# Top-k attention feeding a squared-ReLU feed-forward: half-batch order, 256-row chunks and a contiguous score layout

## The chip, the cores and the metric

The kernel runs on 1 core of one Trainium2 chip. The metric is the device time of one execution in microseconds, as the median of the runs; lower is better.

## The reference

There are 8 batches, 8 heads, 576 positions and a head dimension of 64. Scores are `q k^T / 8`. In each row of 576 scores only those at or above the 32nd largest stay, a softmax runs over them, and the result multiplies `v`. The heads are put side by side into rows of 512 (4608 rows in all), which go through `relu(x @ w_in)^2 @ w_out`, with 2048 hidden columns.

```python
scores = scale * np.matmul(q, k.transpose(0, 1, 3, 2))
kth = np.partition(scores, -top_k, axis=-1)[..., -top_k:-top_k + 1]
scores = np.where(scores >= kth, scores, -1e9)
attn = softmax(scores)
x = (attn @ v).transpose(0, 2, 1, 3).reshape(B * S, H * D)
r = np.maximum(x @ w_in, 0.0)
out = (r * r) @ w_out
```

## The kernel before

**Groups.** Two heads make a pair (four pairs `hp` in a batch). A group is 128 query rows of both heads of one pair, `g` = 0 to 3, or, as group `Z`, the last 64 query rows of two pairs. A batch has 18 groups, the run has 144.

**One group** (`top_k`, L495, then `attend`, L640). PE makes the scores (`scores`, L503, or `scores_z`, L516) into the three PSUM banks of the pool `ps_s`, of which there is one. ACT copies them to SBUF, tile `s`, in two copies (L533 and L535): in PSUM the last 64 keys of both heads lie in the third bank, in SBUF between the two heads. DVE takes the maximum `m` of the two halves of a row (L589: one operand from PSUM, one from SBUF) and the maximum of the halves of `m` (L594, called `big`). POOL makes the matching minima with four integer adds and subtracts (`whole`, L585, shown at L586): `t1`, `t2`, `mid` and `low`. DVE then takes three rounds of 8 maxima and a replacement of them, over 104, 124 and 272 columns (L609, L613), and a last MAX8 over all 576 columns (L616), which gives the 32nd largest, `kth`. ACT makes `w` from `s` and `kth` (L624); PE transposes `s` and adds `w` times a steep constant in two steps (`flip`, L644), so that what is below `kth` goes far negative; ACT takes the exponential of all 1152 columns (L657).

**Groups into rows** (`collect`, L661). PE multiplies by `v`, ACT copies, DVE takes reciprocals (L685), POOL scales (L687), PE transposes, ACT copies into a tile `xt` (or `xz`) of the feed-forward's input (L711). `stages` says which groups of a pair are collected together.

**Feed-forward** (`feed`, L717). A chunk is a list of row ranges in `CHUNKS` (L413 to L419). It starts when the last of its rows has been collected. For a chunk of `nt` rows, `kf = 512 // nt` hidden blocks share one PSUM bank; PE multiplies with `win` (`fh`), ACT takes ReLU (L737), and the square is taken on DVE in the last chunk (L745), on POOL in the chunks that L747 names (L748), on ACT elsewhere (L751). Then PE multiplies 128 rows at a time with `wo` (`fo`), ACT copies (L768), SP stores (L776). Chunks of before: two of 256 rows in batch 0; 512 rows each in batches 1 to 5; 384 rows of all `Z` groups of batches 0 to 5; 512 rows of batch 6; 384 rows of batch 6's `Z`, rows 256 to 511 and the `Z` of batch 7; then 128 and 128 rows of batch 7.

**Order** (`batch_order`, L396). In batch 0 the groups 0 and 1 of all pairs come first, then 2 and 3. In batches 1 to 6 a pair's four groups come together, with a `Z` after every second pair's. In batch 7 `Z` comes first, then groups 2, 3, 0 and 1.

**Planner.** Every instruction group is an `Op` with an engine, an assumed duration and a priority. `schedule` (L120) is a list scheduler: at each moment each engine takes, of what is ready and has its buffers, the smallest priority; `nbf` is an earliest time. Each engine then runs its list in order, with semaphore waits. Priorities come from `tg = T0 + PER * n` for group `n`: scores at `tg - LEAD`, `m` at `tg - ME`, `big` at `tg - MQ`, POOL's `t2` and `mid` at `tg - MP`, the feed-forward at its chunk's time plus `LAG` (`LAGL` in the last batch), in steps of `STEP`. Buffers: 6 of `s`, 3 of `m`, 4 of `f`, 5 of `qk` (the transposed q and k of a pair), 5 of `vb`, and 2 PSUM banks (`psum`) for everything that is neither scores nor transposed scores.

Of the kernel before, what the change touches and what calls it, by code (L numbers as in the profile page):

```python
# [12 lines left out]
P = 128  # L13
# [278 lines left out]
def bass_top_k_attn__then__act_relu_squared_kernel(  # L292
# [20 lines left out]
    def sb(name, shape, dt=FP32, n=None):  # L313
# [13 lines left out]
    LAGL = 10  # L327
    WARM = 0

    ident32 = sb("ident32", [P, P])  # L330
# [24 lines left out]
        "av": ([P, 4, D + 1], FP32, 3), "x": ([P, 4, D], BF16, 2), "xt": ([P, NCT, 512], BF16, 3),  # L355
        "xz": ([P, NCT, 64 * (NB - 2)], BF16, 1), "o": ([P, DM], FP32, 2),
# [9 lines left out]
    ps32 = nc.alloc_psum_tensor("ps", [P, 8, 512], FP32)  # L366
    ps16 = ps32[:, :, :].bitcast(BF16)

    ps_s, ps_e, psum = Pool("ps_s", 1), Pool("ps_e", 1), Pool("psum", 2)
    BASE = {"ps_s": 0, "ps_e": 3, "psum": 6}  # L370

    def tile(nm):
        return Tile(pools[nm])

    def at(t):
        return mem[t.pool.name][t.slot]
# [17 lines left out]
    Z = 4  # L394

    def batch_order(b):  # L396
        if b == 0:
            seq = []
            for gs in ((0, 1), (2, 3)):
                seq += [(hp, g) for hp in range(NHP) for g in gs]  # L400
            return seq + [(0, Z), (2, Z)], [[0, 1], [2, 3]]
        if b < NB - 1:
            seq = []
# [9 lines left out]
    CHUNKS = [[(0, 0, 256)], [(0, 256, 256)]]  # L413
    for b in range(1, NB - 2):
        CHUNKS.append([(b, 0, 512)])
    CHUNKS.append([(b, 512, 64) for b in range(NB - 2)])
    CHUNKS.append([(NB - 2, 0, 512)])
    CHUNKS.append([(NB - 2, 512, 64), (NB - 1, 256, 256), (NB - 1, 512, 64)])
    CHUNKS += [[(NB - 1, 0, 128)], [(NB - 1, 128, 128)]]  # L419
# [7 lines left out]
    def mm(o, l, r, start, stop=True):  # L427
        return pe.matmul(o, l, r, start=start, stop=stop, skip_group_check=True)  # L428
# [4 lines left out]
    def build(full, weights, pl):  # L433
# [7 lines left out]
        def load_pair(b, hp, base):  # L441
# [11 lines left out]

            def loadv():
                r = at(rv)
                res = [nc.sync.dma_start(r[:, 4 * h:4 * h + 4, :], v[b, 2 * hp + h, 0:512, :].rearrange(
                    "(tb p) d -> p tb d", p=P)) for h in range(2)]

                for h, low, e in ((0, 0, 8), (1, 64, 9), (1, 0, 10) if hp % 2 == 0 else (0, 64, 11)):
                    res.append(nc.sync.dma_start(r[low:low + 64, e, :], v[b, 2 * hp + h, 512:576, :]))  # L460
# [34 lines left out]
        def top_k(gi, qks, tg):  # L495

            n = state["n"]
            state["n"] += 1
            ss, st = Tile(ps_s), tile("s")

            def scores():  # L503
                o = wide(ss)
                for h, to, c0, n_ in ((0, 1024, 512, 64), (0, 0, 0, 512), (1, 512, 0, 512), (1, 1088, 512, 64)):
                    x = at(qks[h])
                    if to == 1088:
                        pe.wait_ge(fence, fences[0])
                    ins = mm(o[:, to:to + n_], x[64 * h:64 * h + 64, 0, 128 * gi:128 * gi + 128],
                             x[64 * h:64 * h + 64, 1, c0:c0 + n_], to != 1088)  # L510
                    if to == 1024:
                        fences[0] += 1
                        ins.then_inc(fence, 1)
                return ins

            def scores_z():  # L516
                o = wide(ss)
                for i in range(2):
                    x = at(qks[i])
                    for to, c0, n_, first in ((1024 + 64 * i, 512, 64, i == 0), (512 * i, 0, 512, True)):  # L520
                        for h in range(2):
                            ins = mm(o[64 * h:64 * h + 64, to:to + n_], x[64 * h:64 * h + 64, 0, 512:576],
                                     x[64 * h:64 * h + 64, 1, c0:c0 + n_], first)
                return ins

            qu = sorted(set(qks), key=lambda t: t.num)
            pl.op("pe", 1.25 if gi != Z else 1.4, tg - LEAD, scores if gi != Z else scores_z, r=qu, w=[ss], take=[ss, st])


            def flat():  # L530
                return at(st)[:, :, :].rearrange("p i c -> p (i c)")

            cp = [pl.op("act", 1.1, tg - LEAD + 1, lambda: act.copy(  # L533
                two(flat(), 640, 512), two(wide(ss), 512, 512)), r=[ss], w=[st]),
                pl.op("act", .35, tg - LEAD + 1, lambda: act.copy(  # L535
                    flat()[:, 512:640], wide(ss)[:, 1024:1152]), r=[ss], w=[st])]

            dk = [0]

            def dve(dur, fn, dp=0, **kw):  # L540
                dk[0] += 1
                return pl.op("dve", dur, tg + .33 * dk[0] + dp, fn, **kw)
# [38 lines left out]
            else:  # L581
# [135 lines left out]
        def feed(chunk, xt, tm, step):  # L717
# [74 lines left out]
        for b in range(NB):  # L792
# [3 lines left out]
            for hp, gi in seq:  # L796
# [179 lines left out]
```

## Time and profile before

| what | us |
|---|---|
| median of 3 runs (lowest to highest) | 933.46 (932.37 to 939.02) |
| the profiled execution's own time | 930.32 |
| its span, first to last instruction | 928.2 |

The profiled execution lies 2.1 us above its span and 3.1 us under the median. Times below are microseconds from the start of the span. Busy is the union of an engine's instructions; the mean of a group is the length of one instruction, and neighbours overlap a little, so that sums of means are more than busy time. PEclk is the share of full TensorE clock that was granted.

### The profile page before, as it was taken

How to read it: one execution, taken by the hardware profiler on the slowest of the kernel's cores; microseconds unless marked ns; L12 is line 12 of the kernel's file. 1: busy time of each engine (PE TensorE's matmuls, PEld its weight loads, DVE VectorE, ACT ScalarE, POOL GpSimd, SP SyncE). 2: the span in 40 equal slices, each digit the busy share in tenths (PEclk: the TensorE clock that was granted, in tenths of full speed). 3: DMA queues.
4: the chain of work that ended last, by engine and by line, in shares of the span. 5: the costliest groups of instructions: out<-in, count | busy, mean ns of one | idle time of the engine just before them, and what ended most of it. 6: DMA issues, size and time to landing. Idle time of an engine off the chain costs nothing.

```text
span 928.2 us, 20946 instructions
## 1 busy us (share of the span) xinstructions
PE 810.1 (87%) x7253; PEld 565.7 (61%) x7330; DVE 864.2 (93%) x3269; ACT 742.8 (80%) x1277; POOL 750.3 (81%) x794
## 2 busy tenths in 40 slices
PE   5766889997689999888888898888998999999996
PEld 4555567766465666656566666656666655665664
DVE  3999999999999999999999999999999999998931
ACT  3665898987699878997799977998779789787762
POOL 6998988878777888777877887877899986899961
PEclk9898999999899999999999999999999999999999
DMA  6742521034101222111210131111211010000101
GB/s 138 190 129 91 141 54 53 14 88 91 39 6 37 53 51 63 27 29 49 58 45 16 40 89 37 41 39 39 52 38 26 13 37 13 24 13 1 43 27 38
DMA packets 126978, 48.11 MB, mean 52 GB/s; under 512 B 119184, under 2 KB 119184, under 8 KB 126864
## 3 DMA queue, kind: packets, MB, share of 16 engines
q1 hardware_dynamic: 125664, 46.39, 19.8%
q8 instruction: 59, 0.97, 0.4%
q14 instruction: 55, 0.45, 0.2%
q10 hardware_dynamic: 1200, 0.30, 0.2%
HBM read 37.22 MB, written 9.44 MB: 50 GB/s over the span
## 4 chain that ended last, share of the span: by engine, by line
DVE 45%; PE 35%; ACT 14%; issue 3%; DMA 1%; POOL 1%; SPq 0%; DVEq 0%
PE ps L428 27%; DVE f L613 13%; DVE kth L616 10%; DVE c L609 10%; PE ps L431 9%; DVE m L589 6%; DVE f L594 5%; ACT p L657 5%; ACT w L624 3%; ACT s L533 2%; ACT g L737 1%; ACT g L751 1%; DMA rq<-in_q_dram 1%; ACT xt L711 0%; ACT qk L488 0%
## 5 line engine op out<-in xcount | busy, mean ns | idle before, releaser
L613 DVE MATCH_REPLACE8 f<-c,f 128x104 f32<-128x104 f32 (+2 forms) x864 | 267.2, 317 | 0.4 <-issue 0.3
L609 DVE MAX8 c<-f 128x8 f32<-128x104 f32 (+2 forms) x864 | 243.7, 321 | 0.1
L428 PE MATMUL ps<-qk 64*128 64x64 f32 (+3 forms) x1280 | 213.9, 454 | 32.8 <-DVE m L589 31.6
L624 ACT ACTIVATE w<-s,kth 128x576 bf16<-128x576 f32 x288 | 222.3, 782 | 6.2 <-DVE kth L616 6.1
L586 POOL TENSOR_TENSOR t<-s 128x576 int32<-128x576 int32 x144 | 203.1, 1413 | 17.7 <-ACT s L535 17.6
L431 PE MATMUL ps<-ident,s 128*128 128x128 f32 x1296 | 200.2, 283 | 16.0 <-ACT w L624 15.4
L533 ACT COPY s<-ps 128x1024 f32<-128x1024 f32 x144 | 146.5, 1017 | 84.2 <-PE ps L428 83.8
L616 DVE MAX8 kth<-f 128x8 f32<-128x576 f32 x288 | 203.4, 748 | 1.6 <-POOL f L586 1.6
L586 POOL TENSOR_TENSOR f<-t,f 128x288 int32<-128x288 int32 x144 | 114.4, 795 | 110.8 <-DVE f L594 94.7
L586 POOL TENSOR_TENSOR f<-t,m 128x576 int32<-128x576 int32 x144 | 202.7, 1408 | 0.0
L428 PEld LDWEIGHTS ps<-qk 64*128 64x128 f32 (+1 forms) x1280 | 129.2, 180 | 110.2 <-DVE m L589 48.1
L657 ACT ACTIVATE p<-ps 128x1152 bf16<-128x1152 f32 x144 | 162.9, 1131 | 33.5 <-PE ps L428 32.6
L431 PEld LDWEIGHTS ps<-ident,s 128*128 128x128 f32 x1296 | 147.0, 143 | 50.1 <-ACT w L624 21.1
L428 PE MATMUL ps<-xt,win 128*128 128x512 bf16 (+3 forms) x674 | 126.8, 324 | 13.7 <-ACT g L737 7.4
L428 PE MATMUL ps<-wo,g 128*128 128x512 bf16 x529 | 134.2, 379 | 4.5 <-ACT xt L711 1.2
L589 DVE TENSOR_TENSOR m<-ps,s 128x576 f32<-128x576 f32 x144 | 107.5, 747 | 19.3 <-ACT s L535 16.9
L428 PE MATMUL ps<-steep_bf,w 128*128 128x128 bf16 x1296 | 121.4, 221 | 0.0
L586 POOL TENSOR_TENSOR t<-m 128x288 int32<-128x288 int32 x144 | 115.1, 799 | 0.0
L594 DVE TENSOR_REDUCE f<-m 128x288 f32<-128x576 f32 x144 | 106.7, 747 | 0.1
L737 ACT ACTIVATE g<-ps 128x512 bf16<-128x512 f32 (+1 forms) x152 | 87.2, 581 | 20.2 <-PE ps L428 19.7
L428 PEld LDWEIGHTS ps<-steep_bf,w 128*128 128x128 bf16 x1296 | 98.4, 99 | 3.6
L428 PEld LDWEIGHTS ps<-xt,win 128*128 128x128 bf16 x704 | 57.7, 98 | 51.8 <-ACT g L737 11.8
(57 smaller groups left out, 774.6 us busy)
## 6 DMA issues: line engine op xcount, KB each, us to landing
rq<-in_q_dram SPq DMA_DIRECT2D x64, 128.0 KB, 2.5
rv<-in_v_dram SPq DMA_DIRECT2D x64, 128.0 KB, 2.4
rk<-in_k_dram SPq DMA_DIRECT2D x62, 128.0 KB, 2.6
out_dram<-o SPq DMA_DIRECT2D x31, 256.0 KB, 2.1
g<-in_moe_w_in_dram SPq DMA_DIRECT2D x8, 512.0 KB, 4.7
g<-in_moe_w_out_dram SPq DMA_DIRECT2D x8, 512.0 KB, 3.9
rv<-in_v_dram SPq DMA_DIRECT2D x96, 16.0 KB, 2.2
out_dram<-o SPq DMA_DIRECT2D x10, 128.0 KB, 2.4
```

The lines of the kernel that those rows point to most:

```text
L428: return pe.matmul(o, l, r, start=start, stop=stop, skip_group_check=True)
L431: return pe.matmul(o, i, ident, is_transpose=True, skip_group_check=True, **kw)
L533: cp = [pl.op("act", 1.1, tg - LEAD + 1, lambda: act.copy(two(flat(), 640, 512), two(wide(ss), 512, 512)), r=[ss], w=[st]), pl.op("act", . ...
L586: return pl.op("gp", dur, prio, lambda: gp.tensor_tensor(o().bitcast(I32), x().bitcast(I32), y().bitcast(I32), op), **kw)
L589: dve(.67, lambda: vec.tensor_tensor(at(m)[:, :, :], two(wide(ss), 736, HALF), two(flat()[:, HALF:], HALF, HALF), ALU.max), dp=-ME, r=[ss] ...
L594: big = dve(.67, lambda: vec.tensor_reduce(at(f)[:, :, 0:QUART], at(m)[:, :, :].rearrange("p i (a c) -> p i c a", a=2), AX.X, ALU.max), dp ...
L609: lambda i=i, t=t, c0=c0, c1=c1: vec.max(eighth(t, i), at(f)[:, i, c0:c1]),
L613: lambda i=i, t=t, c0=c0, c1=c1: vec.match_replace(at(f)[:, i, c0:c1], eighth(t, i), at(f)[:, i, c0:c1], NEG), hold=[f])]
L616: ks.append(chain(kth, i, prev[i] + [low], .665, lambda i=i: vec.max(eighth(kth, i), at(f)[:, i, :]), hold=[f]))
L624: pl.op("act", .77, tw + .8 * i, lambda i=i: act.activation(at(wt)[:, i, :], at(st)[:, i, :], ACTF.Relu, bias=kth[:, i, n:n + 1], scale=-1.0),
L657: pl.op("act", 1.15, tt + 1, lambda: act.activation(at(pt)[:, :, :].rearrange("p k q -> p (k q)"), wide(e), ACTF.Exp, scale=0.125), r=[e], ...
L737: return act.activation(at(g)[:, 0:kf * nt], bank(hh)[:, 0:kf * nt], ACTF.Relu)
```

## The change

The order of batches 0 to 6 becomes groups 0 and 1 of all pairs, then 2 and 3 with a `Z` behind every second pair. Chunks become 256 rows (half a batch over all heads), the `Z` rows of four batches make a chunk of 256, and batch 7's groups 2 and 3 are collected together. The scores of a pair stand in PSUM as in SBUF, 1152 columns in a row: head 0 in columns 0 to 575, head 1 in 576 to 1151. So one ACT copy takes the place of two, and the block of 64 and 64 keys that the heads share is now head 0's last and head 1's first keys (loads of `v` follow). The four products are issued alternately for head 0 and head 1: 64 and 128 columns, then 512 and 448, the last behind the fence. `M1` is 0, so the branch under it makes no instructions. The squares go to POOL in batch 7 and for 2 of the 8 tiles of other chunks, to ACT for the rest. The planner's numbers are others.

```diff
-    PER = 6.0
-    LEAD = 20
-    ME = 10
-    MQ = 0
-    MP = 3
-    LAG = 20
-    STEP = 3.2
-    LATE = 1.5
-    LAGL = 10
+    PER = 5.54
+    LEAD = 8.16
+    ME = 11.99
+    MQ = 9.97
+    MP = 1.61
+    SQ = 1.19
+    M1 = 0
+    LAG = 26.67
+    STEP = 3.08
+    LATE = .69
+    LAGL = 17.1
...
-"xt": ([P, NCT, 512], BF16, 3), "xz": ([P, NCT, 64 * (NB - 2)], BF16, 1)
+"xt": ([P, NCT, 256], BF16, 4), "xz": ([P, NCT, 256], BF16, 2)
...
         if b < NB - 1:
-            seq = []
+            seq = [(hp, g) for hp in range(NHP) for g in (0, 1)]
             for hp in range(NHP):
-                seq += [(hp, g) for g in range(4)]
-                if hp % 2 == 0:
-                    seq.append((hp, Z))
+                seq += [(hp, 2), (hp, 3)] + ([(hp - 1, Z)] if hp % 2 else [])
             return seq, [[0, 1], [2, 3]]
-        seq = [(0, Z), (2, Z)] + [(hp, g) for g in (2, 3) for hp in range(NHP)]
-        return seq + [(hp, g) for g in (0, 1) for hp in range(NHP)], [[0], [1], [2], [3]]
+        seq = [(0, Z), (2, Z)] + [(hp, g) for hp in range(NHP) for g in (2, 3)]
+        return seq + [(hp, g) for g in (0, 1) for hp in range(NHP)], [[0], [1], [2, 3]]
...
+    CHUNKS = []
+    for b in range(NB):
+        if b < NB - 1:
+            CHUNKS += [[(b, 0, 256)], [(b, 256, 256)]]
+        if b % 4 == 3:
+            CHUNKS.append([(b - 3 + i, 512, 64) for i in range(4)])
+    CHUNKS += [[(NB - 1, 256, 256)], [(NB - 1, 0, 128)], [(NB - 1, 128, 128)]]
...
-                for h, to, c0, n_ in ((0, 1024, 512, 64), (0, 0, 0, 512), (1, 512, 0, 512), (1, 1088, 512, 64)):
+                for h, to, c0, n_ in ((0, 512, 512, 64), (1, 1024, 448, 128), (0, 0, 0, 512), (1, 576, 0, 448)):
...
-            cp = [pl.op("act", 1.1, tg - LEAD + 1, lambda: act.copy(
-                two(flat(), 640, 512), two(wide(ss), 512, 512)), r=[ss], w=[st]),
-                pl.op("act", .35, tg - LEAD + 1, lambda: act.copy(
-                    flat()[:, 512:640], wide(ss)[:, 1024:1152]), r=[ss], w=[st])]
+            cp = [pl.op("act", 1.2, tg - LEAD + 1, lambda: act.copy(
+                at(st)[:, :, :].rearrange("p i c -> p (i c)"), wide(ss)), r=[ss], w=[st])]
...
-                elif b >= NB - 2 or (b == NB - 3 and len(chunk) > 1):
+                elif last or i * SQ % 8 < SQ:
                     pl.op("gp", ...
```

## Rows read from the trace of the kernel before

**Rows 1.** The page, part 1: engine, busy us, share of the span, instructions.
```profile
PE 810.1 (87%) x7253; PEld 565.7 (61%) x7330; DVE 864.2 (93%) x3269; ACT 742.8 (80%) x1277; POOL 750.3 (81%) x794
```

**Rows 2.** By stretch: length, busy PE, PEld, DVE, ACT, POOL, PEclk, DMA, GB/s.
```profile
400.00:500.00 100.00, 88.91 (x804) 61.66 (x813) 100.00 (x377) 85.68 (x146) 80.12 (x81) 1.00 0.17 42
...
800.00:850.00 50.00, 48.34 (x428) 33.15 (x433) 45.70 (x178) 41.62 (x76) 45.77 (x51) 1.00 0.03 12
850.00:900.00 50.00, 48.21 (x385) 30.62 (x390) 36.88 (x145) 34.28 (x66) 45.81 (x53) 1.00 0.06 22
```

**Rows 3.** DVE's waits from 800 to 900: us in total, times, longest.
```profile
DVE rzall L685 <- ACT av L683: 9.1, 3, 4.2
DVE f L613 <- POOL f L586: 4.1, 5, 1.9
DVE m L589 <- POOL f L586: 2.0, 2, 1.7
DVE kth L616 <- POOL f L586: 1.6, 1, 1.6
```

**Rows 4.** POOL's instructions by line and shape: count, busy us, mean ns.
```profile
L586 POOL TENSOR_TENSOR t<-s 128x576 int32<-128x576 int32 x144 | 203.1, 1413 | 17.7 <-ACT s L535 17.6
L586 POOL TENSOR_TENSOR f<-t,m 128x576 int32<-128x576 int32 x144 | 202.7, 1408 | 0.0
...
L586 POOL TENSOR_TENSOR t<-m 128x288 int32<-128x288 int32 x144 | 115.1, 799 | 0.0
L586 POOL TENSOR_TENSOR f<-t,f 128x288 int32<-128x288 int32 x144 | 114.4, 795 | 110.8 <-DVE f L594 94.7 <-DVE rzall L685 15.7
...
L748 POOL TENSOR_TENSOR g<-g 128x384 bf16<-128x384 bf16 x32 | 26.3, 832 | 3.6 <-ACT g L737 3.6
...
L748 POOL TENSOR_TENSOR g<-g 128x512 bf16<-128x512 bf16 x20 | 20.7, 1039 | 10.6 <-ACT g L737 10.5
```

**Rows 5.** POOL from 887 to 898, in order of time: start, us, and idle before.
```profile
887.07 3.19 POOL L748 TENSOR_TENSOR g<-g 128x384 bf16<-128x384 bf16 x4
...
896.34 1.40 POOL L586 TENSOR_TENSOR f<-t,m 128x576 int32<-128x576 int32 x1
```

**Rows 6.** ACT by line and shape: the two copies of scores, and the exponential.
```profile
L657 ACT ACTIVATE p<-ps 128x1152 bf16<-128x1152 f32 x144 | 162.9, 1131 | 33.5 <-PE ps L428 32.6
...
L533 ACT COPY s<-ps 128x1024 f32<-128x1024 f32 x144 | 146.5, 1017 | 84.2 <-PE ps L428 83.8
...
L535 ACT COPY s<-ps 128x128 f32<-128x128 f32 x144 | 40.7, 282 | 0.0
```

**Rows 7.** PE in order of time: 256-column products, 512-column products, one group's scores.
```profile
132.84 1.92 PE L428 MATMUL ps<-xt,win 128*128 128x256 bf16 x16 [0.79 <-ACT g L737]
...
401.58 1.89 PE L428 MATMUL ps<-xt,win 128*128 128x512 bf16 x8
...
410.10 1.35 PE L428 MATMUL ps<-qk 64*128 64x64 f32 x8 [0.23 <-DVE m L589]
```

**Rows 8.** PE from 800 to 900 by line and shape: the feed-forward's products.
```profile
L428 PE MATMUL ps<-wo,g 128*128 128x512 bf16 x104 | 25.8, 379 | 1.0 <-ACT s L535 0.6
...
L428 PE MATMUL ps<-xt,win 128*128 128x512 bf16 x59 | 15.2, 379 | 0.7 <-ACT av L683 0.4
...
L428 PE MATMUL ps<-xt,win 128*128 128x384 bf16 x64 | 12.4, 327 | 0.6 <-ACT g L737 0.6
```

**Rows 9.** The end, in order of time: the last kth, last product with v, last chunk.
```profile
897.77 1.42 DVE L616 MAX8 kth<-f 128x8 f32<-128x576 f32 x2 [1.59 <-POOL f L586]
...
903.41 1.13 ACT L657 ACTIVATE p<-ps 128x1152 bf16<-128x1152 f32 x1 [0.24 <-PE ps L428]
...
910.24 0.48 PE L428 MATMUL ps<-vb,p 128*128 128x65 bf16 x10
...
914.19 3.75 PE L428 MATMUL ps<-xt,win 128*128 128x128 bf16 x64
...
921.43 0.58 ACT L768 COPY o<-ps 128x512 f32<-128x512 f32 x1 [2.86 <-PE ps L428]
```

More of the change, by code (lines that the diff above doesn't have):

```diff
@@ L303, in bass_top_k_attn__then__act_relu_squared_kernel @@
     HALF, QUART = S // 2, S // 4
+    REST = (512, 0)
     NHP = 4
@@ L316, in sb @@
         return [nc.alloc_sbuf_tensor(f"{name}{i}", shape, dt) for i in range(n)]
-    PER = 6.0
+    PER = 5.54
     T0 = 12.0
-    LEAD = 20
-    ME = 10
-    MQ = 0
-    MP = 3
-    LAG = 20
-    STEP = 3.2
-    LATE = 1.5
-    LAGL = 10
+    LEAD = 8.16
+    ME = 11.99
+    MQ = 9.97
+    MP = 1.61
+    MA = 12
+    SQ = 1.19
[4 more added lines that the diff above has]
+    LAGL = 17.1
     WARM = 0
@@ L354, in bass_top_k_attn__then__act_relu_squared_kernel @@
         "sh": ([P, 2], FP32, 2), "w": ([P, 2, S], BF16, 4), "p": ([P, 9, 128], BF16, 4),
-        "av": ([P, 4, D + 1], FP32, 3), "x": ([P, 4, D], BF16, 2), "xt": ([P, NCT, 512], BF16, 3),
-        "xz": ([P, NCT, 64 * (NB - 2)], BF16, 1), "o": ([P, DM], FP32, 2),
+        "av": ([P, 4, D + 1], FP32, 3), "x": ([P, 4, D], BF16, 2), "xt": ([P, NCT, 256], BF16, 4),
+        "xz": ([P, NCT, 256], BF16, 2), "o": ([P, DM], FP32, 2),
     }
@@ L367, in bass_top_k_attn__then__act_relu_squared_kernel @@
     ps16 = ps32[:, :, :].bitcast(BF16)
-    ps_s, ps_e, psum = Pool("ps_s", 1), Pool("ps_e", 1), Pool("psum", 2)
-    BASE = {"ps_s": 0, "ps_e": 3, "psum": 6}
+    ps_s, ps_q, ps_e, psum = Pool("ps_s", 1), Pool("ps_q", 1), Pool("ps_e", 1), Pool("psum", 2)
+    BASE = {"ps_s": 0, "ps_q": 2, "ps_e": 3, "psum": 6}
     def tile(nm):
@@ L396, in batch_order @@
     def batch_order(b):
-        if b == 0:
-            seq = []
-            for gs in ((0, 1), (2, 3)):
-                seq += [(hp, g) for hp in range(NHP) for g in gs]
-            return seq + [(0, Z), (2, Z)], [[0, 1], [2, 3]]
         if b < NB - 1:
-            seq = []
+            seq = [(hp, g) for hp in range(NHP) for g in (0, 1)]
             for hp in range(NHP):
-                seq += [(hp, g) for g in range(4)]
-                if hp % 2 == 0:
-                    seq.append((hp, Z))
+                seq += [(hp, 2), (hp, 3)] + ([(hp - 1, Z)] if hp % 2 else [])
             return seq, [[0, 1], [2, 3]]
-        seq = [(0, Z), (2, Z)] + [(hp, g) for g in (2, 3) for hp in range(NHP)]
-        return seq + [(hp, g) for g in (0, 1) for hp in range(NHP)], [[0], [1], [2], [3]]
[L413 to L419, printed above, removed]
+        seq = [(0, Z), (2, Z)] + [(hp, g) for hp in range(NHP) for g in (2, 3)]
[7 more added lines that the diff above has]
+    CHUNKS += [[(NB - 1, 256, 256)], [(NB - 1, 0, 128)], [(NB - 1, 128, 128)]]
     def two(ap, step, n_):
@@ L455, in loadv @@
                 r = at(rv)
-                res = [nc.sync.dma_start(r[:, 4 * h:4 * h + 4, :], v[b, 2 * hp + h, 0:512, :].rearrange(
+                res = [nc.sync.dma_start(r[:, 4 * h:4 * h + 4, :], v[b, 2 * hp + h, 64 * h:64 * h + 512, :].rearrange(
                     "(tb p) d -> p tb d", p=P)) for h in range(2)]
                 for h, low, e in ((0, 0, 8), (1, 64, 9), (1, 0, 10) if hp % 2 == 0 else (0, 64, 11)):
-                    res.append(nc.sync.dma_start(r[low:low + 64, e, :], v[b, 2 * hp + h, 512:576, :]))
+                    res.append(nc.sync.dma_start(r[low:low + 64, e, :], v[b, 2 * hp + h, REST[h]:REST[h] + 64, :]))
                 return res
@@ L498, in top_k @@
             state["n"] += 1
-            ss, st = Tile(ps_s), tile("s")
+            ss, st, sq = Tile(ps_s), tile("s"), Tile(ps_q)
             def scores():
                 o = wide(ss)
-                for h, to, c0, n_ in ((0, 1024, 512, 64), (0, 0, 0, 512), (1, 512, 0, 512), (1, 1088, 512, 64)):
+                for h, to, c0, n_ in ((0, 512, 512, 64), (1, 1024, 448, 128), (0, 0, 0, 512), (1, 576, 0, 448)):
                     x = at(qks[h])
-                    if to == 1088:
+                    if to == 576:
                         pe.wait_ge(fence, fences[0])
                     ins = mm(o[:, to:to + n_], x[64 * h:64 * h + 64, 0, 128 * gi:128 * gi + 128],
-                             x[64 * h:64 * h + 64, 1, c0:c0 + n_], to != 1088)
-                    if to == 1024:
+                             x[64 * h:64 * h + 64, 1, c0:c0 + n_], to != 576)
+                    if to == 512:
                         fences[0] += 1
@@ L517, in scores_z @@
                 o = wide(ss)
-                for i in range(2):
+                for i, runs in ((0, [((512, 512, 64), (0, 0, 512)), ((512, 0, 64), (0, 64, 512))]),
+                                (1, [((1024, 384, 128), (576, 512, 64), (640, 0, 384)),
+                                     ((1024, 448, 128), (576, 0, 448))])):
                     x = at(qks[i])
-                    for to, c0, n_, first in ((1024 + 64 * i, 512, 64, i == 0), (512 * i, 0, 512, True)):
+                    for k_ in range(3):
                         for h in range(2):
-                            ins = mm(o[64 * h:64 * h + 64, to:to + n_], x[64 * h:64 * h + 64, 0, 512:576],
-                                     x[64 * h:64 * h + 64, 1, c0:c0 + n_], first)
+                            if k_ < len(runs[h]):
+                                to, c0, n_ = runs[h][k_]
+                                ins = mm(o[64 * h:64 * h + 64, to:to + n_], x[64 * h:64 * h + 64, 0, 512:576],
+                                         x[64 * h:64 * h + 64, 1, c0:c0 + n_], not 576 <= to < 1024)
                 return ins
             qu = sorted(set(qks), key=lambda t: t.num)
-            pl.op("pe", 1.25 if gi != Z else 1.4, tg - LEAD, scores if gi != Z else scores_z, r=qu, w=[ss], take=[ss, st])
-            def flat():
-                return at(st)[:, :, :].rearrange("p i c -> p (i c)")
-            cp = [pl.op("act", 1.1, tg - LEAD + 1, lambda: act.copy(
-                two(flat(), 640, 512), two(wide(ss), 512, 512)), r=[ss], w=[st]),
-                pl.op("act", .35, tg - LEAD + 1, lambda: act.copy(
-                    flat()[:, 512:640], wide(ss)[:, 1024:1152]), r=[ss], w=[st])]
+            pl.op("pe", 1.25 if gi != Z else 1.4, tg - LEAD, scores if gi != Z else scores_z, r=qu,
+                  w=[ss] + ([sq] if M1 else []), take=[ss, st] + ([sq] if M1 else []))
+            cp = [pl.op("act", 1.2, tg - LEAD + 1, lambda: act.copy(
+                at(st)[:, :, :].rearrange("p i c -> p (i c)"), wide(ss)), r=[ss], w=[st])]
             dk = [0]
@@ L587, in whole, with parts, quarter @@
                         o().bitcast(I32), x().bitcast(I32), y().bitcast(I32), op), **kw)
-                dve(.67, lambda: vec.tensor_tensor(
-                    at(m)[:, :, :], two(wide(ss), 736, HALF), two(flat()[:, HALF:], HALF, HALF), ALU.max),
-                    dp=-ME, r=[ss], hold=[st], after=cp, w=[m], take=[m])
+                def parts(a, n_):
+                    return two(wide(ss)[:, a:], S, n_), at(st)[:, :, HALF + a:HALF + a + n_]
+                def quarter():
+                    return two(ps32[:, 2, 128:416], QUART, QUART)
+                if M1:
+                    m1 = dve(.36, lambda: vec.tensor_tensor(quarter(), *parts(QUART, QUART), ALU.max), dp=-ME,
+                             r=[ss], hold=[st, sq], after=cp)
+                    m0 = dve(.36, lambda: vec.tensor_tensor(at(m)[:, :, 0:QUART], *parts(0, QUART), ALU.max), dp=-ME,
+                             r=[ss], hold=[st], after=cp, w=[m], take=[m])
+                    mc = pl.op("act", .45, tg - MA, lambda: act.copy(at(m)[:, :, QUART:HALF], quarter()), hold=[sq],
+                               w=[m], after=[m1, m0])
+                    big = dve(.36, lambda: vec.tensor_tensor(
+                        at(f)[:, :, 0:QUART], at(m)[:, :, 0:QUART], quarter(), ALU.max), dp=-MQ,
+                        hold=[m, sq], after=[m0, mc], w=[f], take=[f])
+                else:
+                    dve(.67, lambda: vec.tensor_tensor(at(m)[:, :, :], *parts(0, HALF), ALU.max), dp=-ME,
+                        r=[ss], hold=[st], after=cp, w=[m], take=[m])
+                    big = dve(.67, lambda: vec.tensor_reduce(
+                        at(f)[:, :, 0:QUART], at(m)[:, :, :].rearrange("p i (a c) -> p i c a", a=2), AX.X, ALU.max),
+                        dp=-MQ, r=[m], w=[f], take=[f])
                 whole(1.38, tg, ALU.add, lambda: at(t1)[:, :, :], lambda: at(st)[:, :, 0:HALF],
                       lambda: at(st)[:, :, HALF:S], r=[st], w=[t1], take=[t1])
-                big = dve(.67, lambda: vec.tensor_reduce(
-                    at(f)[:, :, 0:QUART], at(m)[:, :, :].rearrange("p i (a c) -> p i c a", a=2), AX.X, ALU.max),
-                    dp=-MQ, r=[m], w=[f], take=[f])
                 whole(.77, tg - MP, ALU.add, lambda: at(t2)[:, :, :], lambda: at(m)[:, :, 0:QUART],
@@ L812, in build @@
                 if first:
-                    xts[i] = tile("xz" if len(CHUNKS[i]) > 4 else "xt")
+                    xts[i] = tile("xz" if len(CHUNKS[i]) > 1 else "xt")
                 collect(gi, held[hp, js[0]], (xts[i], col, first), hp, tt)
```

## The prediction

> **What bounds the kernel now.** I read the page's busy shares first, then busy time by stretch, then DVE's waits in the stretches where it is not full, then the other engines there. The reader is to see three things.
>
> First, DVE is the fullest engine, 864.2 us of 928.2 [rows 1], and from 400 to 500 it is busy for the whole 100.00 us [rows 2]; PE, ACT and POOL have 11, 14 and 20 us free there. So in the middle the time is the number of DVE instructions, and what the other engines do is hidden. 864.2 over 144 groups is 6.0 us for a group.
>
> Second, the last batch is otherwise. DVE is busy for 45.70 us from 800 to 850 and 36.88 from 850 to 900 [rows 2], so 17.4 us are idle. Its waits there [rows 3] are 4.1 + 2.0 + 1.6 = 7.7 us for POOL by name, and 9.1 us at reciprocals. These last are POOL's too: the reciprocals stand in DVE's queue ahead of the last MAX8, and that MAX8 still waits 1.59 us afterwards [rows 9] for POOL's subtraction at 896.34, which ran behind a block of four squares at 887.07 and others like it [rows 5]. POOL is busy for 45.77 and 45.81 of 50 us there and PE for 48.34 and 48.21 [rows 2].
>
> Third, the end. The last MAX8 ends at 899.19; the last exponential ends at 904.54, but its product with `v` starts only at 910.24, since PE is working through feed-forward products; the last chunk starts at 914.19 and its copy ends at 922.01 [rows 9]. From the last MAX8 to the end of the span are 29.0 us.
>
> **The change part by part.**
>
> *DVE.* No instruction is added or taken away, as `M1` is 0. `m` still reads two runs of 288 columns from the first two banks. I cost it at 0. `big` gets priority 9.97 us earlier, behind `m`. POOL's `mid` waits for `big`: 94.7 us of POOL's idle time stand there [rows 4]. That idle goes, but in the middle it costs DVE little.
>
> *Score copy.* Two copies of 1017 and 282 ns become one of 1152 columns; the nearest row is the exponential, 1131 ns over the same three banks [rows 6]. ACT gains between 0 (if the two overlap fully at their ends) and 0.168 us for a group, 24 us in all, and I take 0 on the path, since DVE hides it. At the very start the first group gains 0.1 us. If the cover were gone, it could only help.
>
> *Scores interleaved.* One group now takes 1.35 us on PE [rows 7]: a 64-column product, two of 512 on different rows of the array, a 64-column product. Now 64 stands beside 128 and 512 beside 448. Between a gain of 0.25 us (one small product wholly hidden) and a loss of 0.25 us (the fence now stands ahead of a long product, with the transposes of the group before queued behind it) I take a gain of 0.1, 2 us for the last batch's 18 groups. In the middle it hides behind DVE: PE waits for DVE's `m` before scores anyway, 0.23 us in that row.
>
> *256-row chunks.* The first product runs 16 x 256 columns in 1.92 us where before it ran 8 x 512 in 1.89 [rows 7]: nothing lost. `wo`'s products, copies and stores keep their number. The order by half batches holds a pair's `qk` for 13 to 18 groups rather than 5. With five buffers, the fifth holds the next batch's first pair, two come free after group 13 of 18 and two at the batch's end, and the next batch needs them from its 3rd and 7th group; the number of loads on SP's queue is the same. I cost that at 0, with up to 1 us at each of 7 batch ends as the other end.
>
> The Trainium skill, "TensorE: Matmul & The Clock Gate", section "The mechanism", says that a weight load overlaps with running products only where the row group differs; these all use all rows. By that, twice the loads of 98 ns would be exposed, 32 more in a chunk of 256, 3.1 us a chunk and some 10 us in the last batch, and the sum would end near 926. The rows speak against it: 120 ns for a product of 256 columns leaves no room for a load beside it.
>
> *Squares.* Before, POOL squares all tiles of the chunks fed in batch 7, 30.6 us between 800 and 900 (14.5 + 13.0 + 3.1 of the two kinds at 1039 and 832 ns [rows 4]). After: 2 tiles of batch 6's second half, 8 of the `Z` chunk, 8 of batch 7's 256 rows, and 0 to 4 of the next 128: 18 to 22 at 1.04, so 18.7 to 22.9 us. POOL's need in the last batch is then 18 x (1.413 + 1.408 + 0.799 + 0.795) = 79.5 [rows 4], some 6.5 of scaling, and 21 of squares: 107 us, against 18 x 6.0 = 108 of DVE. They are level, where before POOL needed some 10 more. Of DVE's 17.4 idle us I let 2.5 stay; the ends are 0 and 17. What POOL no longer squares falls to ACT, which has 14 us free in 100 [rows 2].
>
> *Feed-forward left at the end.* From 800 to 900 PE spends 25.8 + 15.2 + 12.4 = 53.4 us on it [rows 8], and it is still full until 914. That is batch 6's 512 rows, 384 more, and 128. After the change half of batch 6 is done earlier; 256 + 256 + 256 + 128 rows are left when the last batch starts, at least 128 fewer. 128 rows cost 3.75 (64 products of 128 columns [rows 9]) and 16 products of `wo` of 512 columns at 1.89 / 8 = 0.236 [rows 7], 3.8, so 7.5 us. PE's own chain thus shortens by between 7.5 and 23 us (if a further 256 rows are done before 800): PE reaches the last chunk between 891 and 907, DVE's side would allow it at about 883 + 12 = 895.
>
> **The sum**, on the profiled execution. Last MAX8: 899.2 - 17.4 + 2.5 = 884.3, less 0.1 at the start, less 1 for the small waits elsewhere that an early `big` removes: 883. From there to the end 29.0 before; I take 28, between 23 (the 5.7 us that the last product with `v` waited are gone) and 36 (7.5 more left over). Span 911, own time 913; the profiled execution was 3.1 under the median of the runs, so the median is 916.
>
> **Rivals.**
>
> *PE becomes the last bound of the tail.* DVE gets through sooner, but what it gains is waited for at the end, since PE must do the same products and `LAGL` lets them lie longer. For it: PE busy 97% there, and its backlog decided 910 to 914. Against it: fewer rows left. The drain is then 36 or more, so 924 to 928; I say 926. (The exposed weight loads above would come out the same.)
>
> *POOL keeps the tail.* The squares stay bunched ahead of DVE's last group, and the 17.4 stay: 916 + 13 = 929 to 933, no change. For it: level needs and an engine that works in order. Against: `mid` is no longer held up, and POOL can work ahead.
>
> *Scores come too late (slower).* Scores are now wanted 8.16 / 5.54 = 1.5 groups ahead, before 20 / 6 = 3.3. On PE a block of 16 products or a transposing step may stand ahead of them, and DVE waits in the middle, where it is now full. One block is 1.92 us [rows 7]. If it strikes once in each of 16 half batches, that is 31 us: 947. It decides from nine such losses (17 us). Against it: six buffers of `s`, PE 11% free [rows 2], and a list scheduler that only orders what competes.
>
> *The change does little of what it says*: interleaving gains nothing. That is 2 us of PE and no change of the forecast.
>
> **How the numbers follow.** Forecast (last MAX8 between 880 and 888, drain 23 to 32) 0.60, PE's tail 0.15, POOL's tail 0.13, late scores 0.12. About 1% is what a measurement of this kernel can tell from no change, so 924.1 and 942.8 are the edges. Faster: the forecast's 0.60, 0.10 of PE's tail and 0.04 of POOL's, 0.74. No change: the other 0.05 and 0.09 of these two, and 0.01 of late scores, 0.15. Slower: late scores, 0.11. The range: below, both ends at their best give 911 - 4 - 5 = 902 of span and 907 of median, so 906; above, it reaches to the middle of POOL's tail, 932, and leaves out late scores, the rest of POOL's tail and a little below, less than 2 in 10.
>
> **What would show it.** Right: DVE over 98% busy from 800 until its last MAX8, which ends between 880 and 888; no block of four squares on POOL ahead of a subtraction; POOL's wait for L594 mostly gone; one ACT copy of about 1.13 us; 256-column products at about 0.12 us; scores at 1.1 to 1.35 us. Wrong: DVE idle in the middle behind ACT's copy (late scores); a last MAX8 at 884 with an end above 920 (PE's tail); DVE's reciprocals or MAX8 waiting for POOL by over 10 us (POOL's tail).

## The result, and the profile after

The changed kernel takes 912.05 us (median; 911.0 to 914.13 in 4 runs), against 933.83 for the kernel before beside it: a ratio of 0.9757, interval 0.9721 to 0.9794. That is faster, as forecast (916; range 906 to 932). The profiled execution has a span of 912.2 us and a time of 914.13.

Part of the 22 us goes with the granted TensorE clock, a mean over an execution of its two levels (2.4 GHz and half of that). Over 38 executions of the kernel before, taken beside the experiments, the time falls as it rises, from 939.78 at 0.972 to 927.78 at 0.990; the changed kernel's four had 0.986 to 0.993. At 0.986 the changed kernel took 913.08 (one execution) and the kernel before 926.86 to 930.9 (five), so 14 to 18 us are left at an equal clock.

The page of the changed kernel, part 1 (as [rows 1]). The source lines of a kernel differ from run to run: PE's products are at L428 in the kernel before, and at L425 here.

```profile
PE 830.8 (91%) x7810; PEld 596.4 (65%) x7810; DVE 859.5 (94%) x3265; ACT 733.2 (80%) x1111; POOL 757.9 (83%) x788
```

Its busy times by stretch (as [rows 2]):

```profile
400.00:500.00 100.00, 94.31 (x890) 69.32 (x890) 96.68 (x367) 87.44 (x138) 82.72 (x83) 0.98 0.18 43
800.00:850.00 50.00, 49.16 (x439) 34.26 (x440) 49.39 (x189) 39.05 (x57) 46.35 (x48) 1.00 0.04 12
850.00:900.00 50.00, 47.64 (x513) 35.77 (x512) 40.81 (x162) 38.20 (x66) 35.16 (x39) 1.00 0.09 28
```

DVE's idle time has moved from the last batch into the middle. From 800 to 850 DVE is busy for 49.39 us where it had 45.70, but from 400 to 500 for only 96.68 where it had 100.00, and PE, with 11 us free before, has under 6. (The trace of the kernel before lacks some records, 47 of 576 products with `wo` among them, so PE had somewhat less free there than it shows.) The chain of work that ended last (the page's part 4), before and after:

```profile
DVE 45%; PE 35%; ACT 14%; issue 3%; DMA 1%; POOL 1%; SPq 0%; DVEq 0%
PE 60%; ACT 21%; DVE 13%; POOL 3%; issue 2%; DMA 0%; SPq 0%; POOLq 0%
```

It ran through DVE above all, and now through PE. DVE's waits from 100 to 800 show a kind that the kernel before did not have there:

```profile
DVE rzall L700 <- ACT av L698: 10.0, 22, 1.3
DVE m L605 <- ACT s L532: 1.3, 2, 0.8
```

These are reciprocals that stand in DVE's queue and wait for a product with `v` and its copy. The end, in order of time (as [rows 9]):

```profile
886.02 1.41 DVE L631 MAX8 kth<-f 128x8 f32<-128x576 f32 x2
...
891.67 1.13 ACT L672 ACTIVATE p<-ps 128x1152 bf16<-128x1152 f32 x1 [0.59 <-PE ps L425]
...
894.28 0.48 PE L425 MATMUL ps<-vb,p 128*128 128x65 bf16 x10
...
897.37 3.75 PE L425 MATMUL ps<-xt,win 128*128 128x128 bf16 x64
...
904.61 0.58 ACT L783 COPY o<-ps 128x512 f32<-128x512 f32 x1 [2.86 <-PE ps L425]
```

The last MAX8 ends at 887.43, 11.8 us earlier than before, and 24.8 us lie behind it where 29.0 lay. The product with `v` starts 1.48 us after the exponential, not 5.7. Groups by line and shape (as [rows 4, 6]):

```profile
L583 POOL TENSOR_TENSOR f<-t,f 128x288 int32<-128x288 int32 x144 | 114.6, 796 | 61.1 <-DVE f L607 55.1 <-DVE rzall L700 4.3
L532 ACT COPY s<-ps 128x1152 f32<-128x1152 f32 x144 | 161.8, 1123 | 49.5 <-PE ps L425 48.4
...
L425 PE MATMUL ps<-xt,win 128*128 128x256 bf16 x960 | 120.9, 273 | 2.5 <-ACT qk L485 1.0 <-ACT av L698 0.8 <-ACT g L752 0.5
...
L763 POOL TENSOR_TENSOR g<-g 128x512 bf16<-128x512 bf16 x50 | 52.0, 1041 | 13.0 <-ACT g L752 12.3
```

A score group and a tile of the feed-forward on PE (as [rows 7]):

```profile
414.82 1.51 PE L425 MATMUL ps<-qk 64*128 64x64 f32 x8
416.26 1.05 PE L425 MATMUL ps<-xt,win 128*128 128x256 bf16 x8
```

The copy takes 1.12 us and a 256-column product 0.126 (120.9 us over 960), as forecast. Two signs of the forecast did not come: a score group takes 1.51 us where it took 1.35, outside the 1.1 to 1.35 that I gave, and POOL still waits 55.1 us for the reduce (L607) where it waited 94.7, which is not "mostly gone".

### The profile page after: what moved, and what is told of

The parts are those of the page before. It is cut to its first block, busy times and chain, and to the rows that moved or that the text cites. A ratio compares the mean times of both kernels' runs of the same rounds, so it can differ in the third digit from the quotient of the medians.

```text
span 912.2 us, 21704 instructions
## 1 busy us (share of the span) xinstructions
PE 830.8 (91%) x7810; PEld 596.4 (65%) x7810; DVE 859.5 (94%) x3265; ACT 733.2 (80%) x1111; POOL 757.9 (83%) x788
## 3 DMA queue, kind: packets, MB, share of 16 engines
q8 instruction: 63, 1.03, 0.5%
## 4 chain that ended last, share of the span: by engine, by line
PE 60%; ACT 21%; DVE 13%; POOL 3%; issue 2%; DMA 0%; SPq 0%; POOLq 0%
PE ps L425 46%; PE ps L428 14%; ACT p L672 6%; ACT w L639 4%; DVE f L628 4%; ACT s L532 3%; DVE c L624 3%; ACT g L752 3%; ACT g L766 2%; DVE m L605 2%; DVE kth L631 2%; DVE f L607 2%; POOL f L583 1%; POOL t L583 1%; ACT qk L485 1%
## 5 line engine op out<-in xcount | busy, mean ns | idle before, releaser
L425 PE MATMUL ps<-qk 64*128 64x512 f32 (+8 forms) x1312 | 236.7, 455 | 21.5 <-DVE m L605 20.6
L624 DVE MAX8 c<-f 128x8 f32<-128x104 f32 (+2 forms) x864 | 240.8, 320 | 0.0
L583 POOL TENSOR_TENSOR t<-s 128x576 int32<-128x576 int32 x144 | 203.1, 1410 | 25.2 <-ACT s L532 24.8
L631 DVE MAX8 kth<-f 128x8 f32<-128x576 f32 x288 | 215.9, 751 | 0.0
L428 PE MATMUL ps<-ident,s 128*128 128x128 f32 x1296 | 196.7, 279 | 7.1 <-ACT w L639 6.8
L532 ACT COPY s<-ps 128x1152 f32<-128x1152 f32 x144 | 161.8, 1123 | 49.5 <-PE ps L425 48.4
L428 PEld LDWEIGHTS ps<-ident,s 128*128 128x128 f32 x1296 | 146.2, 143 | 52.0 <-ACT w L639 31.6
L583 POOL TENSOR_TENSOR f<-t,f 128x288 int32<-128x288 int32 x144 | 114.6, 796 | 61.1 <-DVE f L607 55.1
L425 PEld LDWEIGHTS ps<-qk 64*128 64x128 f32 (+1 forms) x1312 | 118.6, 179 | 63.0 <-DVE m L605 24.7
L425 PE MATMUL ps<-wo,g 128*128 128x512 bf16 x576 | 143.6, 379 | 0.7 <-ACT xt L726 0.5
L425 PE MATMUL ps<-xt,win 128*128 128x256 bf16 (+1 forms) x1088 | 128.7, 267 | 2.5 <-ACT qk L485 1.0
L425 PE MATMUL ps<-steep_bf,w 128*128 128x128 bf16 x1296 | 120.3, 220 | 0.0
L425 PEld LDWEIGHTS ps<-xt,win 128*128 128x128 bf16 x1088 | 95.6, 98 | 23.6 <-ACT w L639 4.6
L607 DVE TENSOR_REDUCE f<-m 128x288 f32<-128x576 f32 x144 | 108.4, 753 | 0.1
L425 PEld LDWEIGHTS ps<-steep_bf,w 128*128 128x128 bf16 x1296 | 97.4, 99 | 3.5
L752 ACT ACTIVATE g<-ps 128x512 bf16<-128x512 f32 x144 | 84.7, 601 | 10.6 <-PE ps L425 9.7
```

Of the source, the lines that this page charges most:

```text
L428: return pe.matmul(o, i, ident, is_transpose=True, skip_group_check=True, **kw)
L532: cp = [pl.op("act", 1.2, tg - LEAD + 1, lambda: act.copy(at(st)[:, :, :].rearrange("p i c -> p (i c)"), wide(ss)), r=[ss], w=[st])]
L583: return pl.op("gp", dur, prio, lambda: gp.tensor_tensor(o().bitcast(I32), x().bitcast(I32), y().bitcast(I32), op), **kw)
L607: big = dve(.67, lambda: vec.tensor_reduce(at(f)[:, :, 0:QUART], at(m)[:, :, :].rearrange("p i (a c) -> p i c a", a=2), AX.X, ALU.max), dp ...
L624: lambda i=i, t=t, c0=c0, c1=c1: vec.max(eighth(t, i), at(f)[:, i, c0:c1]),
L631: ks.append(chain(kth, i, prev[i] + [low], .665, lambda i=i: vec.max(eighth(kth, i), at(f)[:, i, :]), hold=[f]))
```

## The experiments

e1 to e7, e11 and e12 alter one part of the changed kernel; e8 to e10 do one part, or two, in the kernel before.

**e1: products not alternating.**

```diff
-((0, 512, 512, 64), (1, 1024, 448, 128), (0, 0, 0, 512), (1, 576, 0, 448))
+((0, 512, 512, 64), (0, 0, 0, 512), (1, 1024, 448, 128), (1, 576, 0, 448))
```

> The changed kernel with the four products of a score in another order: 64 and 512 columns of head 0, then 128 and 448 of head 1. If the alternation itself made a score group dearer on PE (1.51 us against 1.35 before), the group falls back to about 1.35 us and PE is some 20 us less busy. If DVE alone sets the time, the total stays within 3 us of 912; if PE's work counts at the end (its share of the chain is 60%), it falls to 905 to 909.

909.47 us (908.39 to 913.73), ratio 0.9727 (0.9674 to 0.9781): not to be told from the change. The first expectation is a miss, since a group still takes 1.51 us:

```profile
413.39 1.51 PE L425 MATMUL ps<-qk 64*128 64x64 f32 x8
```

But the edit did not change the order in which the products start. Each fp32 product is two matmul instructions, and the two heads use different rows of the array. In the first 0.21 us of a group, e1 (413.39 to 413.60) and the changed kernel (414.82 to 415.03) both show these two lines, and no product of 512 columns:

```profile
L425 PE MATMUL ps<-qk 64*128 64x64 f32 x2 | 0.4, 296 | 0.0
L425 PE MATMUL ps<-qk 64*128 64x128 f32 x1 | 0.4, 373 | 0.0
```

Head 1's 128 columns start 0.01 us after head 0's first 64, although e1's program has head 0's 512 ahead of them. Whether the compiler or the engine brings this about no run shows. So e1 says nothing of the alternation: in both kernels the heads' products start in turn.

**e2: score layout of before** in the changed kernel: the products, the two copies, `m` and the loads of `v` as in the lines with a minus in the diff.

```diff
-for h, to, c0, n_ in ((0, 512, 512, 64), (1, 1024, 448, 128), (0, 0, 0, 512), (1, 576, 0, 448)):
+for h, to, c0, n_ in ((0, 1024, 512, 64), (0, 0, 0, 512), (1, 512, 0, 512), (1, 1088, 512, 64)):
```

> The changed kernel with the score layout of before: two copies on ACT, products of 64, 512, 512 and 64 columns, v loaded as before. If the layout is hidden behind DVE, 909 to 915. If the single copy was worth something on the path, 915 to 925. If the dearer products cost something, 903 to 909.

920.98 us (914.79 to 923.49), ratio 0.9843 (0.9775 to 0.9912). The group is back at 1.35 us, and yet the kernel is slower, by 9 us by medians (all its runs lie above all of the changed kernel's, though the two ratios' intervals overlap). The last MAX8 ends at 892.54. DVE's waits from 0 to 100, then from 100 to 800:

```profile
DVE m L605 <- ACT s L532: 22.3, 9, 12.5
...
DVE m L605 <- ACT s L532: 6.0, 12, 1.3
```

In the changed kernel these are 17.5 and 1.3. With the new numbers and two copies the scores come late.

**e3: squares as before** in the changed kernel.

```diff
-elif last or i * SQ % 8 < SQ:
+elif b >= NB - 2 or (b == NB - 3 and len(chunk) > 1):
```

> The changed kernel with the rule of before for the squares: all tiles of the last two batches' chunks on POOL (44 tiles where the change has 24 in these chunks, 40 with the last chunk's four on DVE). If POOL's squares were what held DVE in the last batch, DVE's idle time from 800 to its last MAX8 comes back, 8 to 17 us, and the time is 920 to 929. If the order by half batches made the gain, 911 to 916.

915.91 us (915.01 to 916.45), ratio 0.9799 (0.9746 to 0.9853): 4 us over the change by medians, with intervals that overlap. DVE's idle time from 800 to its last MAX8 is 8.5 us, where it was 17.4 before and 1.1 in the changed kernel, but it is idle 6.1 us less ahead of 800, and the last MAX8 ends only 1.0 us later (888.46). The test is weaker than meant: with the new chunks the old rule puts 36 squares on POOL, not the 44 or 40 that I expected, and from 800 to the last MAX8 they take 24.8 us, between the 18.7 of the changed kernel and the 30.6 before.

**e4: planner's numbers of before** in the changed kernel.

```diff
-    PER, LEAD, ME, MQ, MP = 5.54, 8.16, 11.99, 9.97, 1.61
-    LAG, STEP, LATE, LAGL = 26.67, 3.08, .69, 17.1
+    PER, LEAD, ME, MQ, MP = 6.0, 20, 10, 0, 3
+    LAG, STEP, LATE, LAGL = 20, 3.2, 1.5, 10
```

> The changed kernel with the planner's numbers of before (PER 6, LEAD 20, ME 10, MQ 0, MP 3, LAG 20, STEP 3.2, LATE 1.5, LAGL 10). If the numbers carry the gain, 922 or more, with POOL's wait for the reduce back at about 95 us. If the order and the squares carry it, 909 to 917; and if the earlier reciprocals (LATE 0.69) cause DVE's 10 us of waits for ACT's copy in the middle, these fall under 3 us.

927.11 us (922.05 to 933.99), ratio 0.9929 (0.9889 to 0.9969). The last MAX8 ends at 902.94. The waits at reciprocals between 100 and 800 do fall, to 0.6 us, but others take their place there:

```profile
DVE f L626 <- POOL f L581: 6.8, 10, 1.5
DVE m L603 <- ACT s L530: 5.1, 6, 2.3
DVE rzall L698 <- ACT av L696: 0.6, 1, 0.6
```

POOL's idle time ahead of its subtraction is back at 95.9 us, 79.1 of it for the reduce. So the numbers are worth 15 us to this kernel by medians, with intervals apart (some 10 where the granted clock is 0.986 or more: 922.05 and 924.44). The next three ask which.

**e5: numbers nudged**: LAG 26.5, STEP 3.1, LEAD 8.3.

> The changed kernel with three of the planner's numbers moved a little (LAG 26.5 for 26.67, STEP 3.1 for 3.08, LEAD 8.3 for 8.16), which has no meaning of its own. It shows how far the time moves when the list scheduler falls into a neighbouring order: if the numbers work by their sizes, 910 to 915; if the order of the change is one lucky draw among many, 914 to 925.

911.76 us (909.93 to 912.29), ratio 0.9764 (0.9704 to 0.9823). This neighbouring order gives the same time; it is one of many.

**e6: reduce late again**: MQ 0 in place of 9.97.

> The changed kernel with MQ 0 in place of 9.97, so that the reduce L594/L607 that POOL's subtraction waits for is planned late, as before. If the early reduce is what spares DVE its waits for POOL, DVE waits for POOL by 5 us or more in all (0 in the changed kernel, 12 before) and the time is 917 to 922. If POOL has room enough, 910 to 914.

917.28 us (915.67 to 920.57), ratio 0.983 (0.9765 to 0.9896). The size came, the reason not: DVE waits for POOL by only 2.5 us in all. It is busier, 862.5 us rather than 859.5, with the same instructions.

```profile
PE 824.6 (90%) x7758; PEld 594.5 (65%) x7810; DVE 862.5 (94%) x3265; ACT 733.5 (80%) x1111; POOL 753.5 (82%) x788
```

DVE in order of time, in the changed kernel and in the kernel before:

```profile
316.70 0.74 DVE L631 MAX8 kth<-f 128x8 f32<-128x576 f32 x1
317.37 0.41 DVE L624 MAX8 c<-f 128x8 f32<-128x104 f32 x2
317.71 0.07 DVE L628 MATCH_VALUE_LOAD f<-c,f 128x8 f32 x1
...
414.81 0.75 DVE L589 TENSOR_TENSOR m<-ps,s 128x576 f32<-128x576 f32 x1
415.48 0.43 DVE L609 MAX8 c<-f 128x8 f32<-128x104 f32 x2
415.88 0.09 DVE L613 MATCH_VALUE_LOAD f<-c,f 128x8 f32 x1
```

From the start of the pair of MAX8 over 104 columns to the value load are 0.34 us in the first and 0.40 in the second. What differs is the instruction ahead of the pair: a last MAX8 in the first, `m` in the second. Over the three traces the step takes 0.34 us by the median behind a last MAX8 (20 times in the kernel before, 131 in the changed kernel, 69 in e6) and 0.39 behind `m` (73 times before) or behind the reduce (41 times in e6, 0.41 by the mean). So the late reduce of e6 falls ahead of these pairs, and 41 times 0.075 us are the missing 3 us. Why DVE takes longer there the rows don't show. As to the time, the 5 us are by medians, with intervals that overlap and ranges that don't; the two profiled executions differ by 2.0.

**e7: scores wanted early**: LEAD 20 in place of 8.16.

> The changed kernel with LEAD 20 in place of 8.16, as before. If a short lead makes scores come late, DVE's waits for ACT's copy fall under 15 us and the time to 908 or less. If scores that run ahead push the feed-forward and the transposes back, the end grows and the time is 915 or more. If the order competes for nothing, 910 to 914.

912.81 us (912.09 to 914.63), ratio 0.9778 (0.9716 to 0.9839): the lead competes for nothing.

**e8: the kernel before with the change's squares.**

```diff
-elif b >= NB - 2 or (b == NB - 3 and len(chunk) > 1):
+elif last or i * 1.19 % 8 < 1.19:
```

> The kernel before with the change's rule for squares alone: 2 of 16 tiles (of 8 in batch 0) on POOL until batch 7's own chunks, ACT for the others. If POOL's squares were the cause of DVE's 17 idle us in the last batch, 8 to 14 us of them go and the time is 919 to 926. If the order by half batches or the planner's numbers are needed for it, 929 to 934.

(The rule gives POOL 3 of 16 tiles, not the 2 that I wrote.) 934.87 us (929.95 to 942.38), ratio 1.0011 (0.9968 to 1.0054): nothing. Yet the cause that I gave is there. DVE is busy for 49.20 us from 800 to 850 (45.70 before), and the last MAX8 ends at 886.06, 13.1 us earlier:

```profile
884.65 1.41 DVE L616 MAX8 kth<-f 128x8 f32<-128x576 f32 x2
```

All of it is given back behind. From there to the end are 48.0 us, not 29.0, and PE's groups in this stretch show what they hold:

```profile
L428 PE MATMUL ps<-wo,g 128*128 128x512 bf16 x83 | 20.1, 379 | 1.9 <-ACT o L768 1.2 <-DVE flag L890 0.5
L428 PE MATMUL ps<-xt,win 128*128 128x384 bf16 x44 | 8.2, 327 | 0.1
L428 PE MATMUL ps<-xt,win 128*128 128x128 bf16 x128 | 8.1, 219 | 0.4 <-ACT av L683 0.4
```

That is 36.4 us of feed-forward. The same view of the kernel before, from its last MAX8 on:

```profile
L428 PE MATMUL ps<-wo,g 128*128 128x512 bf16 x57 | 13.8, 379 | 0.2
L428 PE MATMUL ps<-xt,win 128*128 128x128 bf16 x112 | 6.9, 219 | 0.0
```

And of the changed kernel:

```profile
L425 PE MATMUL ps<-wo,g 128*128 128x512 bf16 x32 | 7.6, 379 | 0.0
L425 PE MATMUL ps<-xt,win 128*128 128x128 bf16 x111 | 6.7, 219 | 0.0
```

20.7 before, 14.3 after. With less on POOL, DVE is done sooner and PE's backlog takes its place.

**e9: the kernel before with order and chunks alone** (`batch_order`, `CHUNKS` and the sizes of `xt` and `xz` of the change).

> The kernel before with the change's order and chunks alone (squares, score layout and the planner's numbers as before). The theory now: the end of the kernel before has two bounds, POOL's squares ahead of DVE and PE's feed-forward left over, and either alone keeps the time. Then the feed-forward after the last MAX8 falls from 32 to some 15 us, POOL's squares still hold DVE in the last batch by 5 us or more, and the time is 920 to 932. If the order alone makes the gain, 910 to 918; if it needs the planner's numbers, 926 or more with DVE waiting for scores and POOL outside the last batch.

915.87 us (914.07 to 916.26), ratio 0.9821 (0.9776 to 0.9866). My theory that either bound alone keeps the time is a miss: this run takes PE's backlog away, leaves the old rule for squares, and makes most of the gain. The last MAX8 ends at 889.63, with 12.6 us of feed-forward and 24.3 us in all behind it. DVE's waits from 100 to 800 are next to nothing; from 800 to 900 POOL still holds it:

```profile
DVE m L582 <- ACT s L528: 1.3, 3, 0.7
...
DVE rzall L678 <- ACT av L676: 6.9, 3, 4.5
DVE m L582 <- POOL f L579: 5.2, 2, 4.8
DVE f L606 <- POOL f L579: 2.5, 2, 1.8
```

**e10: the same with the change's squares too.**

> The kernel before with the change's order, chunks and squares; score layout and planner's numbers as before. If the two bounds of the end are what held the kernel before, 912 to 920, with the last MAX8 under 892 and under 26 us from there to the end. If the planner's numbers carry a share of their own (as the changed kernel with the old numbers, 927, says), 922 to 930 with DVE's losses outside the last batch.

915.0 us (912.01 to 923.89), ratio 0.9835 (0.9761 to 0.991). The last MAX8 ends at 890.21, with 23.6 us behind it. The squares add nothing that can be measured: of DVE's idle time from 800 to the last MAX8 8.8 us stay, where e9 has 10.1.

**e11: reciprocal later**: the changed kernel with LATE 1.5 in place of 0.69.

> The changed kernel with LATE 1.5 in place of 0.69, so that a reciprocal is planned 1.5 us after its copy is due. DVE waits at reciprocals for 18.6 us in the changed kernel, 10 of them in 22 short waits between 100 and 800. If these are pure loss, they fall under 3 us between 100 and 800 and the time is 904 to 909. If PE or POOL takes their place, 910 to 914.

907.95 us (907.08 to 909.28), ratio 0.9738 (0.9693 to 0.9782): 4 us under the change by medians, all runs under all of its runs, though the two ratios' intervals overlap. DVE's waits from 100 to 800:

```profile
DVE m L605 <- ACT s L532: 5.4, 10, 1.3
DVE rzall L700 <- ACT av L698: 1.9, 4, 0.9
```

Of 10.0 us at reciprocals 1.9 stay, and waits for scores take back 4. It is the fastest kernel of this study by the median.

**e12: small product last.**

```diff
-((0, 512, 512, 64), (1, 1024, 448, 128), (0, 0, 0, 512), (1, 576, 0, 448))
+((0, 512, 512, 64), (0, 0, 0, 512), (1, 576, 0, 448), (1, 1024, 448, 128))
```

> The changed kernel with a score's products in the order 64 and 512 of head 0, then 448 (behind the fence) and 128 of head 1, so that the two long ones stand next to each other as before. If the neighbourhood of the two long products made the 1.35 us of before, a score group takes 1.35 to 1.42 us rather than 1.51; if the sizes 448 and 128 or the fence ahead of a long one do it, 1.5 again. The time is 908 to 914 in either case.

934.05 us (930.71 to 938.1), ratio 1.002 (0.9984 to 1.0055). Both expectations are misses: a group takes 1.73 us, and the time is 22 us up. PE in order of time, then DVE's wait from 100 to 800:

```profile
426.69 1.73 PE L425 MATMUL ps<-qk 64*128 64x64 f32 x8
```

```profile
DVE rzall L700 <- ACT av L698: 22.4, 37, 1.8
```

Nothing else is planned otherwise than in the changed kernel, so 0.22 us more in each of 128 groups of this kind, 28 us of PE, put 22 us on the time. In the changed kernel PE's work is no longer hidden. The fence makes head 1's 448 columns wait for head 0's 64, and its 128 columns, which follow them, start last, 1.35 us after the group's first product.

## Why the prediction was right, point by point

**Where the time went.** The last MAX8 ends 11.8 us earlier. DVE's idle time in the last batch (from 800 to the last MAX8) falls from 17.4 us to 1.1; I let 2.5 stay. Outside it, idle time grew by 9.5 us (2.3 before 100, 7.2 between 100 and 800), where I expected 1.1 less. And DVE's busy time up to the last MAX8 fell from 859.4 to 854.4, where I had 0. 16.3 - 9.5 + 5.0 = 11.8. Behind it 4.2 us are gone, where I took 1. In all 16.0 us of span; I had 17. So the sum came right by luck in part: the idle time elsewhere was off by 10.6 us one way, busy time (5.0), the end (3.2) and the last batch (1.4) the other. The last step failed too: I added 3.1 us from the profiled execution to the median, and this time the median is 2.1 below it (912.05 against 914.13; I had 913 and 916). With the spread of the clock in these kernels, one profiled execution does not tell on which side of it the median lies. And DVE has four instructions fewer, not none (3265 for 3269): groups 2 and 3 of the last batch share their reciprocals.

**What bounds it.** DVE in the middle and POOL's squares in the last batch: e8 shows the second, with DVE 13 us earlier from that alone. But I booked the gain to the squares, and e8 and e9 show that the half-batch order carries most of it: alone it gives 915.87, the squares alone nothing. By itself the order takes DVE's idle time in the last batch from 17.4 to 10.1 us; POOL's squares up to the last MAX8 take 26.9 us there, against 30.6, and no run takes the rest apart. Layout and numbers then move idle time rather than remove it: from e10 to the changed kernel it falls by 7.8 us in the last batch and grows by 7.3 ahead of it.

**PE's tail.** The rival was right of the kernel before with less on POOL (e8: 48 us behind the last MAX8). The change escapes it by the term "feed-forward left at the end": 14.3 us of it rather than 20.7.

**Scores interleaved.** The step that failed: I took a gain of 0.1 us for a group, between -0.25 and 0.25, "hidden behind DVE". It measured a loss of 0.16 us, inside the bounds, and it is no longer hidden: the middle is where PE, 94% busy, now makes DVE wait. e12 prices it from 1.51 upwards, at some 0.8 us of time for 1 us of PE. What the way back to 1.35 would be worth with this layout wasn't tried, for want of an order that has it. The rows show where the 0.16 us lie. What PE still runs at the end of a group, in the changed kernel (416.18 to 416.25) and before (411.25 to 411.36):

```profile
L425 PE MATMUL ps<-qk 64*128 64x448 f32 x1 | 0.5, 536 | 0.0
...
L428 PE MATMUL ps<-qk 64*128 64x512 f32 x1 | 0.6, 589 | 0.0
L428 PE MATMUL ps<-qk 64*128 64x64 f32 x2 | 0.3, 244 | 0.0
```

The product that starts last now has 448 columns where it had 64. It starts 0.97 us after the group's first, not 1.03, but PE's next work comes 0.47 us after it, not 0.25.

**The early reduce.** I costed it at 0 on DVE and 1 us of small waits. It is worth 5 us by medians (e6), and 3.0 of DVE's busy time against 2.5 of waits for POOL.

**Planner's numbers.** I treated them as a means. In the kernel with the old layout they are worth nothing that can be told, or less (e10 without them 915.0, e2 with them 920.98, intervals overlapping); with the new layout 15 us (e4). With the old numbers the new layout costs 12 us by medians (e10 to e4). So layout and numbers fit each other, and together add some 3 us to the order and the squares, which lies within the noise. Of the 15 us the early reduce has some 5 (e6), LEAD none (e7), and LATE less than none (e11); the rest isn't taken apart.

**Late scores** did not come (1.3 us between 100 and 800), and LEAD has no part in it (e7).

**The 256-column products.** The rule of the Trainium skill ("TensorE: Matmul & The Clock Gate", section "The mechanism") that a weight load overlaps only with products of another row group (its text there excepts loads into the background weight buffer) would have cost 3 us a chunk. The trace does not agree with the bare rule: 120.9 us for 960 products is 0.126 each, so here the loads of 98 ns lie beside products that use all rows.

## What to carry to other kernels

Freeing one of two full engines can show as nothing in the time (e8): look at what then lies behind the last instruction of the freed engine. The other way round it need not be so: here the change that took that backlog away made most of the gain by itself (e9). A gap-filling stage such as this feed-forward should get its input in halves as early as the order of the main stage allows; what arrives late is left for the end. Before an edit of an order is taken as a test, see in the trace that the starts changed (e1). And when the bound engine waits in its queue at a small instruction that others feed, as these reciprocals, try to plan that instruction later (e11: 4 us by medians).

## What the runs showed of the hardware

The same 1152 columns of a score group, as eight instructions on two halves of the array's rows, took 1.35, 1.51, 1.51 and 1.73 us, by sizes and order; products of the two halves started in turn whether or not the program had them so (e1). The order that put 448 columns behind the fence in third place cost 0.22 us. A pair of MAX8 over 104 columns took 0.34 us to the value load behind it where a MAX8 stood ahead, and 0.39 where `m` or the reduce did. DVE's 3265 instructions took between 858.7 (e11) and 864.4 us (e4) of busy time in kernels that differ only in their order. And the time of the kernel before fell by 12 us between executions with a granted clock of 0.972 and of 0.990.
